# Attention and mixture of experts on one core: w2 loaded in two halves and plain output matmuls, in place of quadrant matmuls

## The chip, the cores and the metric

One core of a Trainium2 chip runs the whole program. The metric is device time in microseconds (us). TensorE (PE; its weight loads are shown as PEld) multiplies matrices into PSUM, VectorE (DVE) and ScalarE (ACT) empty PSUM and do the elementwise work, GpSimd (POOL) issues the loads with its software queue and computes one small power per batch, SyncE (SP) issues the stores.

## What is computed

The input has 8 batches, 8 heads, 576 positions and 64 columns a head. An attention without softmax is normalized and fed to a layer of experts, of which each batch takes exactly one.

```python
kv  = einsum('bhsd,bhse->bhde', k, v)            # 64 x 64 for each head
out = einsum('bhsd,bhde->bhse', q, kv)
x   = out / sqrt(mean(out*out, -1) + 1e-6) * g_norm
x   = heads side by side: (8, 576, 512)
logits = x.mean(1) @ w_gate                      # 8 experts
e      = argmax(logits, 1)                       # one expert for a batch
gate   = softmax(logits)[e]
y      = gate * (relu(x @ w1[e]) @ w2[e])        # w1: 512 x 1024, w2: 1024 x 512
```

With the inputs used here the eight batches choose experts 4, 4, 7, 6, 5, 1, 3, 1. So batches 1 and 7 take weights that are on the chip already.

## The kernel before

All matmuls are in 16-bit floats, cast from 32 bits by the loads. Work is written as steps, and ORDER (L26) lists 367 of them by hand; `emit` (L459) turns each into instructions, and every engine runs its own in that order. A step is named batch, letter, number, and an x for the other of two evacuating engines: 3W1x is step W1 of batch 3. The letters:

- L loads q, k or v of a batch (number 0, 1, 2), 576 KB, on GpSimd's queue (`load_qkv`, L95). Four buffers each.
- T transposes q of a head pair (`s_qt`, L155) into qT; Q (`s_qr`) puts q in another order for that. K makes the 64x64 kv of all heads and casts it into kvb (`s_kv`, L187).
- O computes the attention output of head pairs and squares it on ScalarE; Y copies it from PSUM to the tile o; M takes the mean square with a matmul against constants and ScalarE's reciprocal root; X multiplies everything into xT and sums over positions (`s_x`).
- G0 to G3 do the gate: the logits, the index of the largest (read into a register by GpSimd), the power on GpSimd (L318), the sum and its reciprocal.
- W0 and W1 load w1 and w2 of the expert into one of three slots (`s_w`, L343). From batch 1 on, VectorE first copies the weights from an earlier slot into this one (L354, two halves); from batch 2 on the slot is chosen at run time. The load is then skipped where one of the two batches before had the same expert.
- m0 to m7 are the units of the first layer: 8 matmuls of 288 columns each, and an evacuation with relu to the tile hT (`m_1`, L383). m9 to m16 are halves of the second layer, 4 matmuls of 512 columns, an even number ending a 128-row tile that is scaled and stored (`m_2`, L407, L430). m8 is the last 64 rows, 16 matmuls of 256 columns (L418).
- D is a filler matmul that keeps TensorE's clock up while it would wait (L152). P changes the PSUM pools from the first batch's to the others'.

For batches above 0 O and M treat two head pairs at once (`s_o2`, `s_m2`, `quads`, L215). A pair of heads has a 64x64 kv each, so half of a 128x128 block would be zeros. Here the array is used in four 64x64 quadrants:

```python
for n, rows in ((0, 0), (1, 1), (0, 1), (1, 0)):
    r = slice(64 * rows, 64 * rows + 64)
    for i in range(2):
        e = slice(64 * (rows ^ i), 64 * (rows ^ i) + 64)
        nc.tensor.matmul(outs[n][e, i, 0:HS], lhs(c + n)[r, e],
                         rhs(c + n)[r, i * HS:(i + 1) * HS], start=True, stop=True)
```

The second half of the positions comes out with the two heads swapped, so Y needs three copies (L236 to L238, shown under the helper's line L182), and `s_kv`'s cast (L204) writes each kv twice.

PSUM after batch 0 has two buffers "a" (T, K, O, M, G) and two buffers "m" (the expert layers), two banks each; O and M take both "a" buffers. hT has two buffers. Batch 0 has its own PSUM tags (three "m", two "s") and plain 128x128 matmuls (`s_o`, `s_m`).

Of the kernel before, what the change touches and what calls it, by code (L numbers as in the profile page):

```python
# [24 lines left out]

ORDER = (  # L26
    "0R1x 0R2 0D1 0R0x 0K0 0T0 0T1 0C0 0C1x 0O0 0D1 0D1 0D1 0K1 0K2x 0T3 0C3x 0T2 0O1x "
    "0C2 0K3 0O2 0D1 0M0x 2L0x 0M1x 0M2x 0X0x 0X1x 0O30 0X2 0D1 0D1 2L2x 0M30 0D1 0O31 "
    "0D1 0M31 2L1x 1T0x 0X30x 0X31 1T2 0G1x 0P0 0D1 1T3 1T1 0W0x 1K0 1O0x 3L0 1Y0 0G2x "
    "1Y1x 1M0 2Q0 1X0x 2T0 1O2 1Y3x 1Y2 1X1x 0m0x 2T2x 2T3 3L2 0W1 1M2x 0m4 0G3 1X2x 2K0 "  # L30
    "2T1x 1X3 1G0 0m5 4L0 2O0x 2Y0 0m7 0m3x 1G1 3L1 2Y1x 3Q0 0m2 4L1x 2M0x 4L2 0m1x 3T0x "
    "3T2x 1G2 0m6 2X0x 1W0 2O2 2Y2 1G3 0m13 0m14 1W1x 2Y3x 0m11 3T1x 0m12x 2M2 5L0 1m0 "
    "2X1x 2X2 1m7 2X3x 3K0 3T3x 1m3 2G0 5L1x 1m6 3O0x 3Y0 5L2x 3Y1x 4Q0x 1m2 1m5 4K0 2G1 "
    "1m4 4T0x 2W0 1m1x 3M0 0m8 6L0 4T2x 3X0x 4T3x 0m15 3O2x 3Y2 0m9x 3X1 3Y3x 6L1 0m16x "
    "2G2x 5K0 4T1x 0m10x 6L2x 1m9 2W1x 3M2 2G3 3X2x 1m10x 3X3x 1m8 4O0 4Y1 1m11x 1m12 "
    "4Y0x 2m0x 4M0x 2m3 5Q0x 5T0x 3G0x 2m1 5T1 2m6 5T3x 4X0x 3G1x 2m7 4X1x 1m13x 5T2x 7L0 "
    "1m14x 3W0x 4O2x 4Y2 1m15 4Y3x 1m16x 3G2 6Q0x 2m2 3G3 6K0x 6T0x 3W1x 2m4 2m5 4M2 4X2x "
    "2m11 2m9x 4X3x 6T1x 2m12x 4G0 5O0 5Y0 2m10 5Y1x 2m13 2m14x 4G1 2m15 5M0 4W0x 2m16x "
    "6T2 2m8 5O2 3m0 5Y2 3m1 5X0x 6T3x 3m6 3m7 5Y3 5M2 3m3 3m5 4W1 4G2x 5X1 7L2x 6O0 5X2x "
    "6Y0 3m2x 3m4 6Y1x 5X3 7L1 4m0x 4m1 6M0 7Q0x 4m4x 4G3x 4m5 5G0x 7T0x 4m2 5G1 4m7 6O2x "  # L40
    "3m15x 3m16x 5W0x 3m13 6X0x 6Y2x 3m14 3m11 5W1x 6Y3x 7T2x 3m12 7T3x 6X1 4m3x 6M2 6X2x "
    "5G2x 6X3 6G0x 3m8x 7K0 7T1x 4m6 3m9 3m10 7O0x 7Y0 5G3 4m13x 4m14 4m15 7Y1x 4m16x 6G1 "
    "5m0 5m6 6W0 5m1x 7M0x 4m9 6W1x 6G2x 4m10 5m4x 7O2x 4m8x 7Y2x 5m2x 4m11x 7X0 4m12x "
    "5m7 5m3 7X1x 7Y3 5m5 6m0x 6G3 5m11x 7M2x 7X2x 5m12x 5m9 7X3x 7G0x 5m10 5m15 5m16x "
    "7G1x 6m5 7W0 6m4 5m13x 5m14 7G2x 5m8x 6m6 6m3 7m0 7m6 6m1 7m5 7m7 7m4 7W1 6m2 7m2 "
    "7m3 7G3 6m7 7m1 6m11 6m12x 7m11 7m12 7m15 7m16 7m13 7m14 6m13x 6m14x 7m9 7m10x 6m15 "
    "6m16x 6m9 6m10 6m8 7m8x "
# [4 lines left out]
def kernel(  # L52
# [31 lines left out]
    hp = ctx.enter_context(tc.tile_pool(name="hp", bufs=2))  # L84
# [48 lines left out]
    ones4 = const.tile([P, P], F16)  # L133
    nc.vector.memset(ones4, 1.0 / Dh)
# [20 lines left out]
    def s_qt(b, c, x=False):  # L155
        s = st[b]
        if "qT" not in s:
            s["qT"] = att.tile([P, NP, S], F16, tag="qT", name="qT")
        p32 = psum("s", 2, 1) if first[0] else psum("a")
        pt = p32.bitcast(F16)  # L160
        for j in range(NJ):
            if "qr" in s:
                nc.tensor.transpose(pt[:, 0, j * R:(j + 1) * R], s["qr"][0:R, c, j],  # L163
                                    ident[0:R, 0:R])
                continue
            for i in range(2):
                nc.tensor.transpose(pt[64 * i:64 * i + 64, 0, j * R:(j + 1) * R],
                                    kvq[b][0][0:R, 2 * c + i, j, :], ident[0:R, 0:R])
        s["pt", c] = pt
        if b > 0:  # L170
            s_tc(b, c, x)
# [15 lines left out]
    def s_kv(b, prs):  # L187
        kt, vt = kvq[b][1:3]
        kv = kvb[:, b % 2]
        p32 = psum("s", 2, 1) if first[0] else psum("a")  # L190
        pk = p32[:, 0].rearrange("p (c e) -> p c e", c=NP)
        for c in prs:
            for j in range(NJ):
                for i in range(2):
                    nc.tensor.matmul(pk[64 * i:64 * i + 64, c, 64 * i:64 * i + 64],  # L195
                                     kt[0:R, 2 * c + i, j, :], vt[0:R, 2 * c + i, j, :],
                                     start=(j == 0), stop=(j == NJ - 1))
        cs = slice(prs[0], prs[-1] + 1)
        for i in range(2):
            r = slice(64 * i, 64 * i + 64)  # L200
            if b == 0:
                nc.vector.tensor_copy(kv[r, cs, r], pk[r, cs, r])
            else:
                nc.vector.tensor_copy(  # L204
                    kv[r].rearrange("p c (i e) -> p c i e", i=2),
                    pk[r, :, r].unsqueeze(2).to_broadcast([64, NP, 2, Dh]))
# [5 lines left out]

    def quads(c, outs, lhs, rhs):  # L215
        for n, rows in ((0, 0), (1, 1), (0, 1), (1, 0)):
            r = slice(64 * rows, 64 * rows + 64)
            for i in range(2):
                e = slice(64 * (rows ^ i), 64 * (rows ^ i) + 64)
                nc.tensor.matmul(outs[n][e, i, 0:HS], lhs(c + n)[r, e],  # L220
                                 rhs(c + n)[r, i * HS:(i + 1) * HS], start=True, stop=True)

    def s_o2(b, c):
        s = st[b]
        po = [psum("a") for _ in range(2)]
        quads(c, po, lambda n: kvb[:, b % 2, n, :], lambda n: s["qT"][:, n, :])
        for n in range(2):
            s["sq", c + n] = sm.tile([P, S], F16, tag="sq", name="sq")
            nc.scalar.activation(two(s["sq", c + n]), po[n][:, :, 0:HS], AF.Square)  # L229
            s["po", c + n] = po[n]  # L230

    def s_y(b, c, x):
        s = st[b]
        o = two(sm.tile([P, S], F32, tag="o", name="o"))
        po = s["po", c]
        copy(x, o[:, 0], po[:, 0, 0:HS])  # L236
        copy(x, o[0:64, 1], po[64:128, 1, 0:HS])
        copy(x, o[64:128, 1], po[0:64, 1, 0:HS])  # L238
        s["o", c, None] = o

    def s_m2(b, c):
        s = st[b]
        pm = [psum("a") for _ in range(2)]
        quads(c, pm, lambda n: ones4, lambda n: s["sq", n])
        for n in range(2):
            s["rs", c + n] = sm.tile([P, S], F32, tag="rs", name="rs")
            nc.scalar.activation(two(s["rs", c + n]), pm[n][:, :, 0:HS],  # L247
                                 AF.Abs_reciprocal_sqrt, bias=epsc)

    def s_o(b, c, h=None):  # L250
        s = st[b]
        po = psum("m", 3) if first[0] else psum("a")
        for i in range(2) if h is None else (h,):
            nc.tensor.matmul(po[:, i, 0:HS], kvb[:, b % 2, c, :],
                             s["qT"][:, c, i * HS:(i + 1) * HS], start=True, stop=True)
        po = po[:, :, 0:HS] if h is None else po[:, h:h + 1, 0:HS]
        if not h:
            s["sq", c] = sm.tile([P, S], F16, tag="sq", name="sq")
        nc.scalar.activation(part(s["sq", c], h), po, AF.Square)
        s["o", c, h] = po  # L260

    def s_m(b, c, h=None):
        s = st[b]
        if not h:
            s["rs", c] = sm.tile([P, S], F32, tag="rs", name="rs")
        for hs in ((0,), (1,)) if first[0] and h is None else ((0, 1) if h is None else (h,),):
            pm = psum("s", 2, 1) if first[0] else psum("a")
            for n, i in enumerate(hs):
                nc.tensor.matmul(pm[:, n, 0:HS], ones, s["sq", c][:, i * HS:(i + 1) * HS],  # L269
                                 start=True, stop=True)  # L270
            nc.scalar.activation(two(s["rs", c])[:, hs[0]:hs[-1] + 1], pm[:, 0:len(hs), 0:HS],
                                 AF.Abs_reciprocal_sqrt, bias=epsc)
# [20 lines left out]
    def s_row():  # L293
        s = st[0]
        pg = psum("s", 2, 1)[0:1, 0, 0:E]
# [6 lines left out]
    def s_index(b, pg):  # L302
# [4 lines left out]
        evs.append(nc.gpsimd.value_load(ixs[0:1, b, 0:1], min_val=0, max_val=E - 1))  # L307
# [35 lines left out]
    def s_w(b, i):  # L343
# [3 lines left out]
        if b > 0:  # L347
            if b > 1 and i == 0:
                st[b]["sv"] = nc.vector.value_load(st[b]["src"][0:1, 0:1], min_val=0,
                                                   max_val=NW - 1)  # L350
# [10 lines left out]
        nh = {0: 4, B - 1: 2}.get(b, 1) if i == 0 else 1  # L361
        n = W.shape[3] // nh
        for h in range(nh):
            fs = slice(h * n, (h + 1) * n)
            nc.gpsimd.dma_start(W[:, own, :, fs], (moe_w1, moe_w2)[i][ds(ev, 1), :, fs]  # L365
# [41 lines left out]
    def m_2(b, t, fcs, x=False):  # L407
# [7 lines left out]
        if t == 4:  # L415
# [6 lines left out]
            if last:  # L422
                ot = outp.tile([P, D // 2], F32, tag="ot4", name="ot4")
                scaled(x, ot, po[:, 0, 0:D // 2], b)
                for i in range(2):
                    nc.sync.dma_start(ob[NJ - 1, R - 64:R, i * D // 2:(i + 1) * D // 2],
                                      ot[64 * i:64 * i + 64])
# [31 lines left out]
    def emit(tok):  # L459
# [8 lines left out]
        elif f == "D":  # L468
            warm(psum("s", 2, 1) if first[0] else psum("a"), c)
# [11 lines left out]
        elif f == "C":  # L481
            s_tc(b, c, x)
# [13 lines left out]
        elif f == "Y":  # L496
            s_y(b, c, x)
        elif b > 0 and f in "OM":
            (s_o2 if f == "O" else s_m2)(b, c)
        else:  # L500
            dict(O=s_o, M=s_m, X=s_x)[f](b, c, h)
# [33 lines left out]
```

## Time and profile before

| | us |
|---|---|
| three runs | 209.13, 209.54, 212.11 (median 209.54) |
| the profiled execution | 209.54, its span 207.9 |
| busy in the span: PE, ACT, DVE, POOL | 179.8, 118.6, 118.2, 49.8 |

The span runs from the first instruction to the last; 1.64 us lie around it. A row of a timeline reads: start, duration, engine, line, operation, output<-input, form, count, and in brackets the idle time of the engine before it with what ended it. A row of groups reads: line, engine, operation, names, form, count, busy us, mean ns of one, idle time before them. A row of the chain reads: start, duration, what. PEclk is the clock granted to TensorE, in tenths of full speed or as a share. A busy PE is one with matmuls in flight; since these overlap, the rate is read from a long row of the chain. The DMA queue of the loads moved 26.30 MB, the stores' 10.05 MB with three first loads.

### The profile page before, as it was taken

Reading aid. Unit: us, or ns where it says so; the run is one execution under the profiler, and the core shown is the slowest. Engines: PE = TensorE matmul, PEld = TensorE weight load, DVE = VectorE, ACT = ScalarE, POOL = GpSimd, SP = SyncE. Lnnn points to the kernel's source line nnn. Section 1 sums busy time; section 2 is a strip of 40 time slices with the busy share of each in tenths; the row PEclk is TensorE's granted clock in tenths of the full one; section 3 lists DMA queues with packets and bytes.
Section 4 is the critical chain, followed back from the end, with each engine's and each line's share of the span. In section 5 each row is a group of like instructions: output and inputs, shape, how many; then the busy total and the mean of one; then the engine's idle time right before and its main releaser. Section 6 shows DMA issues by size and latency. Waiting matters only on the chain.

```text
span 207.9 us, 4625 instructions
## 1 busy us (share of the span) xinstructions
PE 179.8 (87%) x1796; PEld 109.9 (53%) x1796; DVE 118.2 (57%) x308; ACT 118.6 (57%) x209; POOL 49.8 (24%) x64
## 2 busy tenths in 40 slices
PE   1678737898999899999898979999949999999990
PEld 0442513576576544667345647474636666874450
DVE  2335456758886778877658785797555367001220
ACT  2437244548878667778676857864624543662120
POOL 7850248002540081024101070140122004000000
PEclk9985855569999999999999999999988999999997
DMA  6999999996999989999999999999999843002554
GB/s 155 195 201 204 203 201 198 204 208 96 165 215 228 181 136 218 252 226 228 230 227 262 231 158 191 186 167 246 252 191 182 177 116 99 20 0 50 146 160 101
DMA packets 37032, 36.94 MB, mean 178 GB/s; under 512 B 2706, under 2 KB 30354, under 8 KB 37010
## 3 DMA queue, kind: packets, MB, share of 16 engines
q0 software_dynamic: 29328, 26.30, 80.6%
q1 hardware_dynamic: 7474, 10.05, 17.0%
q10 hardware_dynamic: 208, 0.29, 0.5%
q8 instruction: 14, 0.23, 0.4%
q14 instruction: 8, 0.07, 0.1%
HBM read 61.88 MB, written 9.44 MB: 343 GB/s over the span
## 4 chain that ended last, share of the span: by engine, by line
PE 47%; DMA 26%; DVE 9%; issue 6%; ACT 6%; POOL 3%; DVEq 0%; POOLq 0%
DMA W<-in_moe_w_dram 23%; PE ps_m L391 18%; PE ps_m L430 16%; DMA vt<-in_v_dram 3%; PE ps_m L418 3%; PE ps_a L220 3%; DVE o L182 3%; PE ps_a L195 2%; PE ps_a L163 2%; DVE W L354 2%; DVE kvb L204 2%; ACT sq L229 1%; ACT rs L247 1%; POOL qt L104 1%; PE ps_s L269 1%
## 5 line engine op out<-in xcount | busy, mean ns | idle before, releaser
L391 PE MATMUL ps_m<-xT,W 128*128 128x288 f16 x512 | 71.6, 294 | 2.1 <-DVE hT L395 1.4
L430 PE MATMUL ps_m<-W,hT 128*128 128x512 f16 x256 | 59.5, 379 | 1.4 <-DMA W<-in_moe_w_dram 0.7
L391 PEld LDWEIGHTS <-W 128*128 128x128 f16 x512 | 49.8, 101 | 19.2 <-issue 4.2
L398 ACT ACTIVATE hT<-ps_m 128x576 f16<-128x576 f32 x51 | 33.1, 650 | 18.3 <-PE ps_m L391 18.1
L430 PEld LDWEIGHTS <-hT 128*128 128x128 f16 x256 | 23.9, 98 | 29.0 <-issue 3.3
L365 POOL DMA_DIRECT2D W<-in_moe_w_dram x20 | 12.5, 626 | 95.3 <-DVE W L354 23.5
L402 ACT ACTIVATE ot<-ps_m,gates 128x512 f32<-128x512 f32 (+1 forms) x22 | 14.3, 649 | 25.0 <-PE ps_m L430 16.4
L404 DVE TENSOR_SCALAR ot<-ps_m,gates 128x512 f32<-128x512 f32 (+1 forms) x18 | 12.4, 688 | 25.8 <-PE ps_m L430 23.5
L354 DVE COPY W<-W 128x2048 f16 (+1 forms) x28 | 19.3, 697 | 12.6 <-DMA W<-in_moe_w_dram 8.4
L182 DVE COPY o<-ps_a 64x288 f32<-64x288 f32 (+1 forms) x42 | 19.1, 455 | 11.3 <-ACT sq L229 10.8
L229 ACT ACTIVATE sq<-ps_a 128x576 f16<-128x576 f32 x28 | 16.6, 649 | 13.8 <-PE ps_a L220 13.8
L247 ACT ACTIVATE rs<-ps_a,epsc 128x576 f32<-128x576 f32 x28 | 19.2, 737 | 9.1 <-PE ps_a L220 9.1
L280 DVE SCALAR_TENSOR_TENSOR xT<-o,gcol,rs 128x576 f16<-128x576 f32 x28 | 22.2, 815 | 3.2 <-ACT rs L247 3.0
L182 ACT COPY o<-ps_a 64x288 f32<-64x288 f32 (+1 forms) x42 | 16.7, 398 | 0.3
L182 ACT COPY qT<-ps_a 128x576 f16<-128x576 f16 x20 | 12.6, 638 | 6.5 <-PE ps_a L163 6.5
L318 POOL TENSOR_TENSOR lg<-base,dl 128x8 f32<-128x8 f32 x8 | 14.1, 1766 | 3.5 <-DVE dl L312 3.3
L395 DVE TENSOR_SCALAR hT<-ps_m 128x576 f16<-128x576 f32 x13 | 9.8, 754 | 6.9 <-PE ps_m L391 6.8
L195 PEld LDWEIGHTS <-kt 96*64 96x64 f16 x384 | 8.7, 125 | 9.4 <-issue 4.6
L163 PE MATMUL ps_a<-ident,qr 96*128 96x96 f16 x144 | 10.9, 218 | 1.8 <-ACT rs L247 1.0
L204 DVE CAST kvb<-ps_a 64x512 f16<-64x512 f32 x14 | 9.6, 687 | 4.3 <-PE ps_a L195 4.2
L163 PEld LDWEIGHTS <-qr 96*128 96x128 f16 x144 | 8.6, 104 | 5.6 <-issue 2.2
L418 PE MATMUL ps_m<-W,hT 128*64 128x256 f16 x128 | 9.2, 293 | 2.7 <-DVE ot L404 2.7
(69 smaller groups left out, 132.0 us busy)
## 6 DMA issues: line engine op xcount, KB each, us to landing
W<-in_moe_w_dram POOLq DMA_DIRECT2D x14, 1024.0 KB, 14.4
out_dram<-ot SPq DMA_DIRECT2D x24, 192.0 KB, 5.3
qt<-in_q_dram POOLq DMA_DIRECT2D x7, 576.0 KB, 13.4
kt<-in_k_dram POOLq DMA_DIRECT2D x7, 576.0 KB, 15.0
vt<-in_v_dram POOLq DMA_DIRECT2D x7, 576.0 KB, 13.4
out_dram<-ot SPq DMA_DIRECT2D x40, 64.0 KB, 5.4
out_dram<-ot SPq DMA_DIRECT2D x16, 128.0 KB, 5.6
W<-in_moe_w_dram POOLq DMA_DIRECT2D x4, 256.0 KB
```

Source lines behind the costliest of these rows:

```text
L163: nc.tensor.transpose(pt[:, 0, j * R:(j + 1) * R], s["qr"][0:R, c, j], ident[0:R, 0:R])
L182: nc.scalar.copy(out, in_) if x else nc.vector.tensor_copy(out, in_)
L229: nc.scalar.activation(two(s["sq", c + n]), po[n][:, :, 0:HS], AF.Square)
L247: nc.scalar.activation(two(s["rs", c + n]), pm[n][:, :, 0:HS], AF.Abs_reciprocal_sqrt, bias=epsc)
L280: nc.vector.scalar_tensor_tensor(out=part(s["xT"][:, c, :], h), in0=s["o", c, h], scalar=gcol, in1=part(s["rs", c], h), op0=ALU.mult, op1= ...
L318: nc.gpsimd.tensor_tensor(lg, base, st[b]["dl"], ALU.pow)
L354: nc.vector.tensor_copy(W[:, own, h * n:(h + 1) * n], W[:, ds(sv, 1), h * n:(h + 1) * n].rearrange("p o c f -> p (o c) f"))
L391: nc.tensor.matmul(ph[:, i, 0:HS], w1[:, c, fb * P:(fb + 1) * P], s["xT"][:, c, i * HS:(i + 1) * HS], start=(c == 0), stop=(c == 3))
L398: nc.scalar.activation(two(s["hT"][:, fb, :]), ph[:, :, 0:HS], AF.Relu)
L402: nc.scalar.activation(out, in_, AF.Copy, scale=gates[:, b:b + 1])
L418: nc.tensor.matmul(po[64 * i:64 * i + 64, 0, 0:D // 2], s["hT"][:, fc, 4 * P:S], w2[:, fc, i * D // 2:(i + 1) * D // 2], start=(fc == 0), ...
L430: nc.tensor.matmul(po[:, 0, :], s["hT"][:, fc, t * P:(t + 1) * P], w2[:, fc, :], start=(fc == 0), stop=(fc == 7))
```

## The change

The two kernels differ in more than the loading of w2: each has its own variant and its own ORDER.

- w2 is loaded in two transfers, each half of the 1024 rows (`i == 1` in `s_w`); w1 is loaded as before.
- `quads`, `s_o2`, `s_m2`, `s_y` and the constants ones4 are gone. O and M take one head pair for all batches, with two 128x128 matmuls of 288 columns on a kv block that has zeros outside its two 64x64 parts. Above batch 0, O copies its output in one 128x576 copy from PSUM to o. The cast of kv writes each head once.
- ORDER has 374 steps, with 17 fillers instead of 10, and other positions. Second-layer units of one batch are all ahead of the first-layer units of the next; before, those of batches 6 and 7 were mixed.
- hT has one buffer.
- Batch 0's PSUM tags are "t" and "kv" (a bank each), "m" (two of two banks) and "p" (one of two banks); M of a half pair uses the bank of "t" or "kv". C always copies on VectorE.
- The two register loads leave out the check of bounds at run time.
- The last piece of the last batch is stored by the queues of SP and ACT, one each.

```diff
-    hp = ctx.enter_context(tc.tile_pool(name="hp", bufs=2))
+    hp = ctx.enter_context(tc.tile_pool(name="hp", bufs=1))
...
-        for i in range(2):
-            r = slice(64 * i, 64 * i + 64)
-            if b == 0:
-                nc.vector.tensor_copy(kv[r, cs, r], pk[r, cs, r])
-            else:
-                nc.vector.tensor_copy(
-                    kv[r].rearrange("p c (i e) -> p c i e", i=2),
-                    pk[r, :, r].unsqueeze(2).to_broadcast([64, NP, 2, Dh]))
+        nc.vector.tensor_copy(kv[0:64, cs, 0:64], pk[0:64, cs, 0:64])
+        nc.vector.tensor_copy(kv[64:128, cs, 64:128], pk[64:128, cs, 64:128])
...
+    def s_o(b, c, h=None, x=False):
+        s = st[b]
+        po = (psum("p", 1) if h == 1 else psum("m")) if first[0] else psum("a")
         for i in range(2) if h is None else (h,):
             nc.tensor.matmul(po[:, i, 0:HS], kvb[:, b % 2, c, :],
                              s["qT"][:, c, i * HS:(i + 1) * HS], start=True, stop=True)
...
         nc.scalar.activation(part(s["sq", c], h), po, AF.Square)
+        if b > 0:
+            o = two(sm.tile([P, S], F32, tag="o", name="o"))
+            copy(x, o, po)
+            po = o
         s["o", c, h] = po
...
+        pm = (psum("p", 1) if h is None else psum("tkv"[h:2 * h + 1], 1, 1)) if first[0] \
+            else psum("a")
+        for i in range(2) if h is None else (h,):
+            nc.tensor.matmul(pm[:, i if h is None else 0, 0:HS], ones,
+                             s["sq", c][:, i * HS:(i + 1) * HS], start=True, stop=True)
...
-        evs.append(nc.gpsimd.value_load(ixs[0:1, b, 0:1], min_val=0, max_val=E - 1))
+        evs.append(nc.values_load(
+            ixs[0:1, b, 0:1], engines=(mybir.EngineType.Pool,), min_val=0, max_val=E - 1,
+            skip_runtime_bounds_check_because="it is the index of the largest of E values"))
...
-        nh = {0: 4, B - 1: 2}.get(b, 1) if i == 0 else 1
+        if i == 1:
+            for h in range(2):
+                cs = slice(4 * h, 4 * h + 4)
+                nc.gpsimd.dma_start(W[:, own, cs], moe_w2[ds(ev, 1), h * F // 2:(h + 1) * F // 2]
+                                    .rearrange("o (c p) d -> p (o c) d", p=P), cond=cond)
+            return
+        nh = {0: 4, B - 1: 2}.get(b, 1)
...
-                    nc.sync.dma_start(ob[NJ - 1, R - 64:R, i * D // 2:(i + 1) * D // 2],
-                                      ot[64 * i:64 * i + 64])
+                    eng = nc.scalar if i and b == B - 1 else nc.sync
+                    eng.dma_start(ob[NJ - 1, R - 64:R, i * D // 2:(i + 1) * D // 2],
+                                  ot[64 * i:64 * i + 64])
```

The new ORDER around the steps that the prediction speaks of (the end of batch 0's attention, and where batches 3 to 6 take their weights):

```
0W0x 2L1x 0P0x 0D1 1T1 1T2 1T3 0D1 0D1 0D1 0D1 0D1 0W1 0D1 2Q0x 0D1 0G2x 1K0 2T0x 1O0 1O2
1M0 0G3 0m0 2T2 1O1 0m3x 3L0x 3L1 1M1 1X0x 1O3 0m4 0m5 1X1 1M2 1M3x 0m1 1X2 0m7 ...
...
6L1x 2m5 5T0 4M3 3W0x 2m1 2m2 3G2x 4X1x
...
5O0x 2m9x 6L2x 3W1 2m10x 2m15x 2m16x 5O1 4G0 5T2x 6Q0 5M0x 2m11x 2m12x 4G1 3m0 6T0x 7L0x
3m5 6T1x 4W0 3m7x 3m6 5X0x 6T2x
...
4W1x 5X3x 3m12 6O0 5G0x
...
6O2 4m4 5W0x 6X0x 4m3 6O3 5G3 5W1x 4m6 6M2x 4m9x
...
6G1x 5m0 5m4x 6W0 6G2x 5m7
...
5m12x 6W1 5m15x 7M2x 5m16x 7M1 5m8
```

## The prediction

> **What bounds the kernel now.** I read the busy slices first, then windows of the span, then the timeline where a window falls short, then the chain and the groups.
>
> ```profile
> PE   1678737898999899999898979999949999999990
> ...
> PEclk9985855569999999999999999999988999999997
> DMA  6999999996999989999999999999999843002554
> ```
>
> TensorE is the bound, except for its first fifth, where it runs at half clock, and for a notch in slice 30. The DMA engines are full until slice 31: loads are nearly as scarce as matmuls. The same by stage (after the stretch: busy PE, PEld, DVE, ACT, POOL, then granted clock, DMA share, GB/s):
>
> ```profile
> 24.72:45.20 20.48, 15.39 (x177) 9.57 (x177) 11.67 (x29) 9.21 (x17) 7.93 (x9) 0.50 1.34 202
> ...
> 151.00:158.00 7.00, 4.26 (x37) 2.94 (x35) 2.71 (x4) 2.32 (x5) 2.56 (x2) 0.76 1.06 206
> 158.00:203.20 45.20, 45.11 (x318) 27.85 (x315) 15.10 (x36) 18.72 (x31) 2.10 (x4) 1.00 0.45 101
> ```
>
> From 158 us on TensorE works through a backlog without a gap (45.11 of 45.20), so whatever lets it reach that point earlier shortens the time one for one. What is lost lies in the half-clock stretch before 45.2 and in the notch. The notch in the timeline:
>
> ```profile
> 151.73 0.44 PE L220 MATMUL ps_a<-qT,kvb 64*64 64x288 f16 x8
> ...
> 152.77 1.42 DVE L354 COPY W<-W 128x2048 f16 x2 [3.21 <-DMA W<-in_moe_w_dram]
> 154.10 0.75 DVE L404 TENSOR_SCALAR ot<-ps_m,gates 128x512 f32<-128x512 f32 x1
> 154.90 1.92 PE L418 MATMUL ps_m<-W,hT 128*64 128x256 f16 x16 [2.74 <-DVE ot L404]
> ```
>
> Step 6W1 copies w2 from a slot chosen at run time, so it waits for 5W1's load. VectorE runs in order: behind the copy stand the evacuation of an output tile and that of a hidden tile, so TensorE's two "m" buffers stay full and it waits 2.97 us from one matmul's end to the next start. The clock then falls to half for one window of 3.4 us (0.76 over the 7 us): another 1.7 us. That load took this long, and the backlog runs at these rates:
>
> ```profile
> 135.90 16.84 DMA W<-in_moe_w_dram
> ...
> 174.54 12.85 PE ps_m L391 x104
> 187.39 13.81 PE ps_m L430 x64
> ```
>
> So one 288-column matmul at full clock is 12.85/104 = 123.6 ns and a 512-column one 215.8 ns. (The 294 and 379 ns of the groups are latencies of overlapped matmuls.)
>
> **The change part by part.**
>
> *Quadrants removed.* What does a quadrant group cost TensorE's stream?
>
> ```profile
> 116.38 2.13 PE L391 MATMUL ps_m<-xT,W 128*128 128x288 f16 x16
> ...
> 118.44 0.44 PE L220 MATMUL ps_a<-qT,kvb 64*64 64x288 f16 x8
> ...
> 118.82 2.13 PE L391 MATMUL ps_m<-xT,W 128*128 128x288 f16 x16
> ```
>
> From start to start of the plain groups 2.44 us pass; 16 x 123.6 = 1.98 are theirs, so eight quadrant matmuls cost 0.46 us, most of it entering and leaving the mode. The plain form is four 128x288 matmuls, 0.49 us. Over 28 groups (7 batches x 2 pairs x output and mean square) removal costs 28 x 0.03 = **+0.8 us**. Bounds: 0 (the same) and 28 x (0.49 - 0.37) = 3.4, if only the 0.37 us between 118.44 and 118.82 counted; I take 0.8, since the start-to-start row holds all of it.
>
> The Trainium skill, page "TensorEngine Tiling (Array Packing)", sections Tiling Modes and Theoretical Speedup, speaks against this part: four independent 64x64 tiles, up to 2x per small dimension. By it, as an estimate, a group would take a quarter of eight plain matmuls, 0.25 us, and removing 28 would cost 6.8 us instead of 0.8; its own remark that a change of mode drains the array is what the row shows.
>
> *Evacuation.* Three copies a head pair become one:
>
> ```profile
> L182 DVE COPY o<-ps_a 64x288 f32<-64x288 f32 (+1 forms) x42 | 19.1, 455 | 11.3 <-ACT sq L229 10.8
> ...
> L182 ACT COPY o<-ps_a 64x288 f32<-64x288 f32 (+1 forms) x42 | 16.7, 398 | 0.3
> ...
> L395 DVE TENSOR_SCALAR hT<-ps_m 128x576 f16<-128x576 f32 x13 | 9.8, 754 | 6.9 <-PE ps_m L391 6.8
> ...
> L204 DVE CAST kvb<-ps_a 64x512 f16<-64x512 f32 x14 | 9.6, 687 | 4.3 <-PE ps_a L195 4.2
> ```
>
> The copies take 19.1 + 16.7 = 35.8 us. The nearest rows for one 128x576 copy are L395 (0.75) and ScalarE's L398 (0.65): 20 x 0.75 + 8 x 0.65 = 20.2 instead of 35.8 us. The kv casts halve in width: from 0.22 us for 64 columns (L202) and 0.69 for 512, 256 cost 0.42, so 5.9 instead of 9.6 us. This is off the critical path (both engines are 57% busy); its worth is in PSUM. A pair held both "a" buffers for squares and copies (1.19 + 1.22 us to the end); one head pair holds one for 0.65 + 0.75. Stalls over 0.2 us for such reasons (48, 51, 57, 72, 85 us and others) sum to about 5 us after 45 us; I take **-0.5**, because the single steps also come more often. Bounds: -3 and +14 (see the third rival).
>
> *New order, middle.* I sum matmul durations between a load's step and the first step that needs it, before and after, in us of matmul work. Where the profile waits: 5W1 to copy 6W1, 16.2 becomes 21.8; 3W0 to copy 4W0, 14.2 becomes 15.7; 3W1 to 4W1, 19.1 becomes 21.2; 4W0 to its first use, 11.9 becomes 17.1. Shorter: 5W0 to first use 14.5 to 12.4; 4W1 to copy 5W1 14.0 to 13.2; 3W0 to first use 16.7 to 13.0. A load lands 8.5 (least) to 16.8 us after issue; 1 MB alone takes 5.2 us at the 202 GB/s above. What stands ahead in the new queue is one q, k or v load (576 KB, 2.9 us) or none, so I expect 8.5 to 10.5 us, 2.5 to 4 us of slack at the shortest. Then the notch (2.97 + 1.7) goes, and with it the waits at 99.06 us (0.97, w2 landing) and at 120.67 us (1.54: VectorE behind copy 4W1). That is 7.2; I keep 1.2 for new small waits: **-6.0**. Bounds: -7.2 and -1.3 (a notch of 4.7 comes back). If the cover is gone, the price is that notch.
>
> *w2 in halves.* GpSimd issues eight more loads, 0.77 to 0.9 us each for the six batches that load, 0.04 for the two whose expert is already there: 5 us on an engine 24% busy, whose next work is qkv loads and the power L318. Units on the first half can start 2.6 us sooner; nobody waits there in the sum. **0**; bounds -1 and +1. On GpSimd's queue 0W0 now stands ahead of 2L1 and 0W1 ahead of batch 3's loads: w2 of batch 0 lands some 5 us sooner, k of batch 2 some 5 us later, at about 37 us, where 2K0 comes after 45. SP's queue keeps its order of outputs.
>
> The Trainium skill, page "DMA: Bandwidth & Descriptors", section Anatomy of one DMA, speaks against it: about 2.0 us fixed per transfer. By it, as an estimate, six more transfers would add 12 us to the queue. Here queued loads run at 195 to 206 GB/s in every slice from 5 to 45 us whatever their size (144 to 1024 KB), so no fixed part shows.
>
> *Front and warm-up.* The first batch has other PSUM tags and squares sooner: step by step (last v at 13.85 us, q of batch 1 at about 17, two half-pairs in separate banks) I reach the index 0.4 us earlier, and the loads without bounds checks save 0.2 us each. Seven more filler matmuls, six of them ahead of 1K0, push 1K0 from 24.7 to about 28 us at 0.45 us each. But from 1K0 to the first expert unit 0m0 it took 10.4 us (24.66 to 35.10); with single steps it is K 1.5, casts 0.85, output 0.5, square 0.65, copy 0.75, mean 0.5: 5 us. So 0m0 starts at 33 instead of 35.1, the next unit at 36 instead of 39.8, and TensorE is dense from there, so the clock may rise one or two windows before 45.2. **-2.0**; bounds +3.1 (seven fillers, nothing regained) and -5 (clock up at 38.4).
>
> *Smaller.* hT has one buffer, so the first evacuation of batch b+1 waits for the last second-layer matmul of b; it stands behind that in TensorE's order anyway: 0, else one evacuation, 0.75 us a batch. The bounds checks leave VectorE (0.2 us x 6): 0. The last output piece goes on ACT's queue beside SP's: four SP issues take 2.39 us at the end, one is saved: **-0.6**.
>
> Sum on the profiled execution: 207.9 + 0.8 - 0.5 - 6.0 + 0 - 2.0 - 0.6 = 199.6 us of span. It lasted 209.54, which is the median too; with the 1.64 around the span the forecast is **201.2 us**.
>
> **The rivals.**
>
> 1. *A load is late elsewhere.* 3W0 or 5W0 misses its unit, or 5W1's copy blocks VectorE. For: DMA is at 9 tenths, slack 2.5 to 4 us. Against: less stands ahead of each than before. One notch: 201.2 + 4.7 = 205.9.
> 2. *Quadrants were worth their face value* (0.25 instead of 0.46): 201.2 + 28 x 0.21 = 207.1. Against: the start-to-start row. Or the front gives 3.1 up instead of gaining 2.0: 206.3.
> 3. *Slower: single steps starve on PSUM.* 56 output and mean steps take one of two "a" buffers each; an output step holds it 1.4 us. Where less matmul work than this lies before the next but one, TensorE stalls some 0.5 us. With 28 stalls: 201.2 + 14 = 215. It decides from 25 stalls (12.5 us). Against: the new order puts a unit of 0.99 us between most; I find some ten too short.
> 4. *The clock rises at 38.4 us and nothing new waits*: 201.2 - 3 - 1.2 = 197.
> 5. *The change does nothing*: no; every gain here is from waits of the old order, but if they all return, 209.
>
> **How the numbers follow.** Forecast 0.46 (own range 198.5 to 204.5), rival 1 0.20, rival 2 with the front 0.12, rival 3 0.12, rival 4 0.10; rival 5 lies within 1 and 2. About 2%, 4.2 us, is what a measurement of this kernel can tell from no change, so faster means under 205.3: forecast, rival 4 and a fifth of rival 1, 0.60. Slower means over 213.7: rival 3, 0.12. The rest, 0.28, is the same. The range reaches from 197 over rivals 1 and 2 to 208.5, leaving out rival 3 and a little at both ends.
>
> **What would show it.** No DVE wait for a W load beyond 1 us and no notch in PE after 100 us; granted clock up before 45.2 us; 28 fewer mode changes at equal TensorE pace; o copies near 20 us in all. I am wrong if half clock lasts beyond 50 us, if PE waits for W, or if it waits for "a" buffers in more than ten places.

## The result, and the profile after

| | median us | runs | ratio to the kernel before |
|---|---|---|---|
| before | 209.33 | 4, 207.31 to 212.11 | 1 |
| after | 196.0 | 4, 194.46 to 198.61 | 0.937 [0.925, 0.949] |
| after, on another chip | 196.69 | 6, 193.38 to 197.36 | 0.940 [0.931, 0.949] |

The kernel became 6.3% faster. The direction was forecast, but the time lies 1 us below the range's low end and 5 us below the forecast. Ratios here leave out the executions that took over 1.5% longer than the fastest of the same kernel (the profiled one of after and four of the six on the other chip among them), while medians hold all. The profiled execution of after is the longest of its four (198.61 us, span 197.0) and has the lowest mean clock of them, 0.954 against 0.982 to 1.0: TensorE's clock was half from 21.97 to 39.03 us in it, and its front is read with that in mind.

The busy slices of the profile after, then the windows that were read before (stretch: busy PE, PEld, DVE, ACT, POOL, then granted clock, DMA share, GB/s):

```profile
PE   0277799799899999999989999999999999999991
...
PEclk9999755599999999999999999999999999999999
DMA  6999999999999999999999999999999899063035
```

```profile
24.72:45.20 20.48, 18.66 (x170) 12.23 (x171) 10.82 (x26) 8.07 (x13) 9.32 (x11) 0.65 1.27 190
...
98.00:122.00 24.00, 23.42 (x237) 15.82 (x235) 16.44 (x42) 14.94 (x25) 8.76 (x9) 1.00 1.20 226
...
151.00:158.00 7.00, 7.00 (x51) 3.94 (x49) 3.52 (x7) 4.87 (x8) 1.53 (x2) 1.00 0.92 167
```

The notch is gone: in 151 to 158 us TensorE is busy for 7.00 us instead of 4.26, at full clock. The same stretch of the middle in the kernel before shows that more than the notch went: from 98 to 122 us TensorE was busy for 21.23 us, now for 23.42.

```profile
98.00:122.00 24.00, 21.23 (x188) 12.23 (x186) 16.48 (x41) 17.44 (x31) 4.43 (x5) 1.00 1.14 228
```

All waits of TensorE between 45 us and the end of after that are put down to data or buffers (what waits, for what, us in total, times, longest):

```profile
PE ps_a L224 <- DVE o L179: 0.9, 2, 0.5
PE ps_m L358 <- DMA W<-in_moe_w_dram: 0.8, 1, 0.8
PE ps_a L207 <- DVE o L179: 0.5, 1, 0.5
```

Before, the longest of these waits, and that of VectorE's copies of weights, were:

```profile
PE ps_m L418 <- DVE ot L404: 2.7, 1, 2.7
PE ps_m L391 <- DVE hT L395: 1.4, 1, 1.4
PE ps_m L430 <- DMA W<-in_moe_w_dram: 0.7, 1, 0.7
PE ps_a L195 <- issue: 0.7, 2, 0.4
PE ps_a L220 <- DVE qT L182: 0.6, 1, 0.6
```

```profile
DVE W L354 <- DMA W<-in_moe_w_dram: 8.4, 4, 3.2
```

After, one weight load is still late, by 0.8 us, and three waits of about half a microsecond are for the copy of the output out of PSUM. VectorE's copies of weights, which waited 8.4 us for landings before, start without such a wait now; one in the timeline:

```profile
116.87 1.42 DVE L315 COPY W<-W 128x2048 f16 x2
```

To see where the time came from I counted the matmul work done by fixed moments: matmuls started by then, times the full-clock prices of the prediction (all work: 160.6 us before, 161.4 with plain matmuls). One profiled execution each; the kernels of the experiments are there for later. The prices are not exact: the last kernel does 106.1 us of work in the 105.8 between 45.2 and 151 us.

| us of work done by | 45.2 us | 98 us | 151 us | TensorE's end | span |
|---|---|---|---|---|---|
| before | 13.9 | 63.4 | 112.9 | 203.1 | 207.9 |
| after | 15.4 | 68.0 | 119.9 | 193.0 | 197.0 |
| before, plain matmuls and one copy | 17.4 | 66.3 | 116.0 | 196.7 | 201.5 |
| the same with three copies | 16.2 | 65.0 | 114.7 | 198.2 | 203.0 |
| before, plain, no weight copies | 19.3 | 70.0 | 120.9 | 191.7 | 196.7 |
| after, without seven fillers | 19.5 | 72.0 | 125.6 | 187.3 | 191.3 |

Between 45.2 and 151 us, 105.8 us of time, before does 99.0 us of work and after 104.5. So the old middle was 7 us short of what TensorE can do, and the new one 1.3 us.

The first column depends on the execution too. The profiled one of before has a mean clock of 0.921, while the runs of before beside the experiments have medians near 0.95, so part of its late start may be its own. Two more profiled executions speak for the new order: the changed kernel's second (196.61 us, on the other chip) and that with w2 in one transfer (195.29 us, below) are ahead of before by about 4.6 and 5.3 us of work at 45.2 us, and do about 4.7 and 5.7 us more than it between 45.2 and 151.

The other count is of what TensorE loses after 45 us: the stalls over 0.2 us, each the time from one matmul's start to the next less its full-clock price. A stall is put to late weights where TensorE waits for a load, or for VectorE while that works without a pause behind a copy that waited for one.

| us of stalls after 45 us | late weights | others |
|---|---|---|
| before | 6.3 | 5.1 |
| after | 1.1 | 2.1 |
| after, on another chip | 2.2 | 2.1 |
| before, plain matmuls and one copy | 6.2 | 2.1 |
| the same with three copies | 3.0 | 4.0 |

Before lost another 1.7 us to the half clock behind its notch.

### The profile page after: what moved, and what is told of

It is laid out like the page before. It is cut to its first block, busy times and chain, and to the rows that moved or that the text cites. A ratio compares the mean times of both kernels' runs of the same rounds, so it can differ in the third digit from the quotient of the medians.

```text
span 197.0 us, 4393 instructions
## 1 busy us (share of the span) xinstructions
PE 176.1 (89%) x1691; PEld 115.9 (59%) x1691; DVE 111.4 (57%) x289; ACT 106.6 (54%) x168; POOL 54.3 (28%) x72
## 4 chain that ended last, share of the span: by engine, by line
PE 74%; DMA 13%; DVE 4%; ACT 4%; issue 2%; POOL 0%; DVEq 0%; POOLq 0%; ACTq 0%
PE ps_m L358 30%; PE ps_m L398 24%; DMA W<-in_moe_w_dram 5%; DMA qt<-in_q_dram 4%; DMA kt<-in_k_dram 4%; PE ps_a L224 3%; PE ps_a L207 3%; PE ps_a L160 3%; ACT sq L212 3%; PE ps_a L192 3%; DVE o L179 3%; PE ps_m L385 2%; PE ps_a L149 2%; PE ps_kv L149 1%; DVE W L315 1%
## 5 line engine op out<-in xcount | busy, mean ns | idle before, releaser
L358 PE MATMUL ps_m<-xT,W 128*128 128x288 f16 x512 | 69.3, 289 | 0.8 <-DMA W<-in_moe_w_dram 0.8
L369 ACT ACTIVATE ot<-ps_m,gates 128x512 f32<-128x512 f32 (+1 forms) x26 | 17.0, 655 | 18.1 <-PE ps_m L398 11.7
L228 ACT ACTIVATE rs<-ps_a,epsc 128x576 f32<-128x576 f32 x28 | 20.5, 740 | 7.5 <-PE ps_a L224 7.5
L179 DVE COPY o<-ps_a 128x576 f32<-128x576 f32 x20 | 15.0, 756 | 14.6 <-ACT sq L212 14.3
L315 DVE COPY W<-W 128x2048 f16 (+1 forms) x28 | 19.3, 695 | 1.4 <-DVE src L296 0.5
L371 DVE TENSOR_SCALAR ot<-ps_m,gates 128x512 f32<-128x512 f32 (+1 forms) x14 | 9.4, 673 | 18.4 <-PE ps_m L398 16.6
L325 POOL DMA_DIRECT2D W<-in_moe_w_dram x16 | 9.2, 577 | 36.0 <-PE ps_m L398 16.6
L332 POOL DMA_DIRECT2D W<-in_moe_w_dram x12 | 7.0, 588 | 38.8 <-PE ps_m L358 14.7
L179 ACT COPY qT<-ps_a 128x576 f16<-128x576 f16 x15 | 9.5, 636 | 14.2 <-PE ps_a L160 14.2
L224 PE MATMUL ps_a<-sq,ones 128*128 128x288 f16 x56 | 11.3, 291 | 2.0 <-DVE o L179 1.9
L207 PE MATMUL ps_a<-qT,kvb 128*128 128x288 f16 x56 | 11.9, 302 | 1.1 <-DVE o L179 0.7
L224 PEld LDWEIGHTS <-ones 128*128 128x128 f16 x64 | 6.1, 100 | 8.0 <-issue 3.2
```

The source lines that it names most:

```text
L179: nc.scalar.copy(out, in_) if x else nc.vector.tensor_copy(out, in_)
L207: nc.tensor.matmul(po[:, i, 0:HS], kvb[:, b % 2, c, :], s["qT"][:, c, i * HS:(i + 1) * HS], start=True, stop=True)
L224: nc.tensor.matmul(pm[:, i if h is None else 0, 0:HS], ones, s["sq", c][:, i * HS:(i + 1) * HS], start=True, stop=True)
L228: nc.scalar.activation(part(s["rs", c], h), pm[:, 0:2 if h is None else 1, 0:HS], AF.Abs_reciprocal_sqrt, bias=epsc)
L315: nc.vector.tensor_copy(W[:, own, h * n:(h + 1) * n], W[:, ds(sv, 1), h * n:(h + 1) * n].rearrange("p o c f -> p (o c) f"))
L358: nc.tensor.matmul(ph[:, i, 0:HS], w1[:, c, fb * P:(fb + 1) * P], s["xT"][:, c, i * HS:(i + 1) * HS], start=(c == 0), stop=(c == 3))
```

## The experiments

The theories were these. *Late loads*: the time came from the new order, in which copies and matmuls no longer wait for weights; copies on VectorE spread the wait to others. *Form*: it came from the plain matmuls with a lighter evacuation, whatever the order. *Clock*: it came from TensorE's clock rising sooner, through fillers or a denser front. And the part that the change is named after, w2 in halves, might be worth something by itself. Ratios are to the kernel before on the same chip.

**The named part: w2 in one transfer again** (after, edited).

```diff
-            for h in range(2):
-                cs = slice(4 * h, 4 * h + 4)
+            for h in range(1):
+                cs = slice(0, 8)
```

> The changed kernel with w2 of each batch in one transfer, as before. The forecast gave the halves nothing: 196.0 within 1 us. Rival: units on the first half start 2.6 us sooner and the copies behind half a load wait less, so one transfer costs 2 to 4 us: 198 to 200. Other rival, a fixed 2 us per transfer: 12 us less queue time, a gain of 1 us or more where TensorE waits for a load at 142 us.

Measured: 196.8 us (194.37 to 198.42), against 196.0 (194.46 to 198.61) and 196.69 (193.38 to 197.36) for the changed kernel itself. Loading w2 in two halves makes no difference that these runs can tell.

**Old order without the copies of weights on VectorE** (before, edited; it leaves out the copies of batches 2 to 6, whose result the inputs used here never need, since these batches all load).

```diff
-            for h in range(2):
+            for h in range(2 if b in (1, B - 1) else 0):
```

> The kernel before without VectorE's copies of weights for batches 2 to 6 (ten pairs of copies of 0.70 us less, 14 us of VectorE work; with these inputs none of those batches repeats an expert, so the copies carry nothing that is used). Theory A, late loads hold VectorE: the waits of the copies for landing loads at 98, 107, 116 and 149.5 us (8.4 us in sum) no longer stand ahead of evacuations; the notch at 152 us with its half clock goes. 209.3 - 6 to -8 = about 202. Theory B, the middle was gained by lighter evacuation (one copy of 128x576 instead of three, one PSUM buffer held instead of two): only VectorE's relief shows, 209.3 - 2 = 207.

Measured: 204.03 us, 0.980 [0.970, 0.990]: some 4 us faster, less than the 6 to 8 of the late loads and more than the 2 of the form. The notch is gone (first fence), but with no copy to wait, TensorE itself now waits for the same kind of load (second fence, the timeline):

```profile
151.00:158.00 7.00, 7.00 (x61) 4.97 (x58) 3.81 (x9) 4.88 (x10) 0.00 (x0) 1.00 1.13 206
```

```profile
121.01 2.13 PE L391 MATMUL ps_m<-xT,W 128*128 128x288 f16 x16 [1.81 <-DMA W<-in_moe_w_dram]
```

So the copies made the late loads dearer, but the loads are late without them too.

**New order without these copies** (after, the same edit; it leaves out the same).

> The changed kernel without the copies of batches 2 to 6 (with these inputs they carry nothing that is used). Theory A: its profile shows one wait on a weight load in the middle (0.99 us at 142 us, TensorE itself, not behind VectorE), so nothing is left to gain: within 1 us of 196.0. Theory B says the same within 2 us. If it gains over 3 us, copies still cost in the new order and A is wrong about where they stopped costing.

Measured: 195.4 us, 0.942 [0.933, 0.950]. No gain that can be told: no copy waits for a load in the new order.

**Old order with plain matmuls and one copy** (before, edited: in `s_o2` and `s_m2`, and the kv cast and `s_y`).

```diff
-        quads(c, po, lambda n: kvb[:, b % 2, n, :], lambda n: s["qT"][:, n, :])
+        for n in range(2):
+            for i in range(2):
+                nc.tensor.matmul(po[n][:, i, 0:HS], kvb[:, b % 2, c + n, :],
+                                 s["qT"][:, c + n, i * HS:(i + 1) * HS], start=True, stop=True)
...
-        copy(x, o[:, 0], po[:, 0, 0:HS])
-        copy(x, o[0:64, 1], po[64:128, 1, 0:HS])
-        copy(x, o[64:128, 1], po[0:64, 1, 0:HS])
+        copy(x, o, po[:, :, 0:HS])
```

> The kernel before with its own order and its pairs, but with plain 128x128 matmuls for output and mean square, one 128x576 copy for three, and kv cast once. TensorE pays 28 x 0.03 = 0.8 us. Theory A: the late loads stay, so the time does too: 209.3 +0.8 -0.5 to -2, some 208.5. Theory B: the gain of the middle comes along: 209.3 - 3 or more, 206 or less. Rival (quadrants at face value, 0.25 us a group): 209.3 + 6, 215.

Measured: 202.67 us, 0.971 [0.962, 0.979], about 6 us faster with the old order. By the table of work (one execution each), 3.5 us of it are gained by 45.2 us; the clock rises for good at 38.47 us instead of 45.2. The middle gains nothing (98.6 us of work in it, 99.0 before), since the notch now falls into it, and the rest comes after 151 us. By the stalls, those for late weights stay (6.2 us) and the others fall from 5.1 to 2.1. The loads are as late as ever, with new places to wait at:

```profile
PE ps_m L429 <- DMA W<-in_moe_w_dram: 2.2, 1, 2.2
PE ps_m L390 <- DVE xT L279: 1.9, 1, 1.9
PE ps_m L417 <- DVE ot L403: 1.6, 1, 1.6
```

The second and third stand behind a waiting weight copy on VectorE. The third is the notch itself, now before 151 us, shorter and without a fall of the clock:

```profile
147.73 1.42 DVE L353 COPY W<-W 128x2048 f16 x2 [2.35 <-DMA W<-in_moe_w_dram]
149.07 0.74 DVE L403 TENSOR_SCALAR ot<-ps_m,gates 128x512 f32<-128x512 f32 x1
...
149.86 1.06 PE L417 MATMUL ps_m<-W,hT 128*64 128x256 f16 x16 [1.59 <-DVE ot L403]
```

**The same, but with three copies a head pair** (`copy(x, o[:, 0], ...)` and two copies of 64 rows, from the rows where the plain form has them). This parts the evacuation from the matmuls.

> The old order with plain matmuls and kv cast once, but still three copies from PSUM for each head pair. It splits the 5.6 us that the plain form gave. If the three copies and the buffers they hold were the cause (theory B): back to about 207. If leaving the quadrant mode or the halved casts were: it stays near 203. By the steps of the prediction, the first stretch needs 0.5 to 0.65 us less for each pair's copies, twice on the way to 0m0: I expect 204.5.

Measured: 204.11 us, 0.988 [0.981, 0.996]. So both parts of the form gain: the one copy in place of three, and the plain matmuls with the narrower cast of kv, which the two kernels share. How much is whose is not settled: the ratios put the copies at 1.7% of 2.9% (the two intervals do not meet, but come from two chips), the medians at 1.4 us (204.11 less 202.67) and the profiled spans at 1.5, of which the table of work shows 1.2 by 45.2 us. In the stalls of the two profiled executions, three copies lose 4.0 us outside the late weights, one copy 2.1.

**Each quadrant group twice** (before, edited; it repeats work and changes no value). This prices the quadrant mode.

```diff
-        for n, rows in ((0, 0), (1, 1), (0, 1), (1, 0)):
+        for n, rows in 2 * ((0, 0), (1, 1), (0, 1), (1, 0)):
```

> The kernel before with each group of eight quadrant matmuls issued twice in a row (sixteen, the same result): it prices the quadrant matmuls apart from entering and leaving the mode. If the prediction's reading holds (most of the 0.46 us is the change of mode), eight more inside the mode cost eight steps of the 157 ns seen for seven steps plus the second wave, 0.24 us: 28 x 0.24 = 7 at most, less where TensorE waits: 209 + 4 to 7. Rival, 0.46 us is the price of the matmuls themselves: 28 x 0.46 = 13, 221.

Measured: 207.95 us, 1.008 [1.004, 1.012]. In the timeline a group now has 16 matmuls:

```profile
116.41 2.13 PE L391 MATMUL ps_m<-xT,W 128*128 128x288 f16 x16
118.48 0.68 PE L220 MATMUL ps_a<-qT,kvb 64*64 64x288 f16 x16
119.09 2.13 PE L391 MATMUL ps_m<-xT,W 128*128 128x288 f16 x16
```

2.68 us pass from plain group to plain group; less 16 x 123.6 ns that is 0.70 us (0.71 over all groups), where eight matmuls took 0.46. Eight quadrant matmuls by themselves are 0.245 us, and going into the mode and out of it 0.22 us. The surprise is the total: 28 x 0.245 = 6.9 us of added TensorE work cost 0.8%, 1.7 us (at most 2.5 by the interval; 1.0 by the medians, 207.95 against 206.94). The work filled time in which TensorE had been waiting: between 45.20 and 151 us it was busy for 103.28 us instead of 100.02, and its stalls after 45 us sum to 4.5 us instead of the 11.4 before. Nor does a better clock show that could have paid for it: over the executions that the ratio is taken from, the mean clock has a median of 0.946, and 0.949 in the kernel before on the same chip. The weight copies on VectorE, which now come later, waited only 4.4 us instead of 8.4, and the notch did not come:

```profile
DVE W L354 <- DMA W<-in_moe_w_dram: 4.4, 4, 1.4
```

A kernel that TensorE alone bounds in its middle could not do that.

**Both: old order, plain form, no weight copies.**

> The old order with plain matmuls and light evacuation, and without the weight copies of batches 2 to 6 (which carry nothing that is used with these inputs). Alone the two edits gave 5.6 and 4.2 us. If one acts in the first 45 us and in keeping the clock up, the other on late loads behind VectorE, they add up but for the 1.7 us of half clock that both remove: 208.2 - 8 = 200. What then is left to the new kernel (196) is the order of the middle, the fillers and the end: some 4 us. Rival, both remove the same waits: 202.

Measured: 199.31 us, 0.967 [0.959, 0.974]. The two gains, 2.0% and 2.9%, should give 4.9% if they were independent; it is 3.3% (the interval of the form alone, 0.962 to 0.979, holds it). So in part they remove the same waits.

**Plain old order with half of each load of weights of batches 2 to 6** (it leaves out the second half of w1 and of w2, so these units compute with old weights; the number of matmuls is the same). This asks directly what late loads cost, those of q, k and v behind them included.

```diff
+            if 1 < b < B - 1:
+                fs = slice(0, n // 2)
```

> The old order with plain matmuls and light evacuation (0.971 of before), and only half of each weight load of batches 2 to 6 (the other half is left out, so what is multiplied there is old data): 5 MB, some 26 us of the load queue less. Theory A, what this order still loses after 45 us is late loads (waits on a weight load of 2.4 us at 94, 2.1 at 116 and 1.8 at 148 us in its profile): 202.7 - 5 to -6, 0.945 of before. Rival, the order of the attention steps against the expert units: it stays at 0.965 to 0.971.

Measured: 197.17 us, 0.953 [0.947, 0.959], 1.8% below the plain old order with whole loads. The middle does 104.6 us of work, as the changed kernel's does. No wait of TensorE for weights is left:

```profile
PE ps_a L195 <- DMA vt<-in_v_dram: 0.6, 1, 0.6
```

**The changed kernel with the same halves left out.**

> The changed kernel with the same halves of weight loads left out. Theory A: its order has loads early enough, only waits of up to 1 us are left: 196.0 - 0 to -1. Rival, loads bound the new order as well, only less: 3 us or more.

Measured: 194.73 us, 0.935 [0.926, 0.945], against 0.937 and 0.940 for the whole loads. In the new order the loads cost no time that can be told: 1 us at most by the ratios, though intervals of 1% either way could hide 2.

**Fewer fillers** (after, without seven of the eight between 0P0 and 1K0), **the same again, and no fillers at all** (all 17 left out, which stand ahead of 1K0; they compute nothing that is used).

```diff
-    "0X30 0D1 0D1 0X31x 0G1x 0W0x 2L1x 0P0x 0D1 1T1 1T2 1T3 0D1 0D1 0D1 0D1 0D1 0W1 0D1 "
-    "2Q0x 0D1 0G2x 1K0 2T0x 1O0 1O2 1M0 0G3 0m0 2T2 1O1 0m3x 3L0x 3L1 1M1 1X0x 1O3 0m4 "
+    "0X30 0D1 0D1 0X31x 0G1x 0W0x 2L1x 0P0x 0D1 1T1 1T2 1T3 0W1 "
+    "2Q0x 0G2x 1K0 2T0x 1O0 1O2 1M0 0G3 0m0 2T2 1O1 0m3x 3L0x 3L1 1M1 1X0x 1O3 0m4 "
```

> The changed kernel without seven of its eight filler matmuls between the first batch's attention and 1K0. Theory C, fillers hold the clock: TensorE falls to half clock from about 22 to 42 us in every run, 2 to 5 us slower than 196.0. Rival, the fillers only push 1K0 back (it comes at 31.0 us in the profile, 27.8 where the clock was up): without them 1K0 comes 2 to 3 us sooner and the time falls by 1 to 3 us.

> The changed kernel without seven fillers ahead of 1K0, once more: if they only push 1K0 back, 1 us under the changed kernel on the same chip; if they hold the clock, 1 us or more above it.

> The changed kernel without any of its 17 filler matmuls. Without seven of them it took 195.0, no slower. Theory C, fillers hold the clock up: half clock from the start to about 40 us, 198 to 200. Rival, the chain of batch 0 and 1 bounds the first 35 us and TensorE's clock matters little there: 194 to 196.

Measured: 194.96 us, 0.947 [0.938, 0.955]; again 195.44 us, 0.942 [0.936, 0.948]; without any 194.87 us, 0.944 [0.936, 0.952]. The changed kernel, run again on the chip of the second of these:

> The changed kernel itself, beside the next one on one chip: 0.94 of before, 195 to 196.

Measured: 196.69 us, 0.940 [0.931, 0.949]. Fillers neither bring the gain nor cost any of it that can be told. Whether a denser front brings some of it through an earlier clock was not tried by itself.

**The smaller parts undone** (after, with the bounds checks back, two hT buffers, and the last piece stored by SP alone).

> The changed kernel with its small parts undone: run-time bounds checks back, hT with two buffers, the last piece stored by SP alone. The forecast gave the store 0.6 us and the others nothing: 196.0 + 0.6, at most +1.5 if the checks (0.2 us each, twice a batch, behind them the weight copies) lie on a path.

Measured: 196.89 us, 0.947 [0.938, 0.957]. These parts are worth 0.7% to 1.0% by the ratios, and as the interval holds the changed kernel's ratio, this is not settled.

**Some of these parts on the old order** (plain, no weight copies, with loads of registers unchecked and the last piece on two queues).

> The old order with plain matmuls, without the weight copies of batches 2 to 6, and with the new kernel's small parts (unchecked register loads, last piece stored by two queues). Without the small parts it took 0.967 of before. If the small parts are worth what undoing them in the new kernel cost (1 us at most): 0.962 to 0.965. Then 4 us up to the new kernel belong to the order alone. If they carry more of the rest: 0.955 or less.

Measured: 198.64 us, 0.959 [0.953, 0.966], where 0.967 [0.959, 0.974] was without them. The intervals overlap: under 1%, not settled.

No version was clearly faster than the changed kernel.

## Why the prediction was wrong in size

The step that failed is the worth of the lighter evacuation. The sum has it at -0.5 us, as off the critical path; the stalls that it stands for fell by 3.0 us, and together with the plain matmuls it gave about 6 us in the old order, where the sum has +0.8 - 0.5. The other miss is the front, whose size changes from one execution to the next.

*The bound (failed in part).* "TensorE is the bound, except for its first fifth" and the notch held from 158 us on, where the backlog is. From 45 to 151 us it held only in the main. TensorE was busy there in nine slices of ten, but 3.3 us went to late weights and 5.1 to other stalls. Doubling the quadrant groups showed that 6.9 us more work cost 1.7 us, and halving the loads of the plain old order gave 1.8%.

*Quadrants removed, +0.8 (right).* The mode's price is 0.46 us a group as read, of which 0.22 is entering and leaving: about half, and not "most of it". The plain form is 0.49:

```profile
43.01 0.49 PE ps_a L224 x4
```

The Trainium skill, page "TensorEngine Tiling (Array Packing)", section Key Properties, says that a change of tiling mode drains TensorE, without a price; the doubled groups give it here, 0.22 us. Without that, the eight quadrant matmuls (0.245 us) would have been twice as fast as the plain four.

*Evacuation, -0.5 (the step that failed).* The copies fell from 35.8 us to 20.1, where 20.2 was worked out:

```profile
L179 DVE COPY o<-ps_a 128x576 f32<-128x576 f32 x20 | 15.0, 756 | 14.6 <-ACT sq L212 14.3
```

```profile
L179 ACT COPY o<-ps_a 128x576 f32<-128x576 f32 x8 | 5.1, 635 | 0.0
```

What they are worth was mis-sized. The prediction found about 5 us of TensorE's stalls after 45 us that go back to buffers of PSUM and took 0.5 of them. By the count of stalls outside late weights, they were 5.1 us and are 2.1 after, in both profiled executions, so the term measures -3.0 us, its own bound. It is the form that does it: in one profiled execution each, the old order with plain matmuls has 4.0 with three copies and 2.1 with one. Plain matmuls and light evacuation, +0.8 - 0.5 = +0.3 in the sum, gave 2.9%, about 6 us, by themselves in the old order, of which one copy for three is between 1.4 us and over half. What goes beyond the stalls I had called "off the critical path". By the table of work (one execution each) it was on the path in two more places: in the chain of batch 1's attention, which decides when the dense stretch begins, and around the notch, where VectorE's queue is what TensorE waits for. The prediction had both places, but as gains of the order.

*New order, middle, -6.0 (right in size).* The waits that it names, 7.2 us with the half clock, are gone. Kept back for new ones was 1.2 us; one late load, at 143.14 us, cost 1.1 in the first profiled execution of after, and two cost 2.2 in the second. One wait more went than listed, 0.82 us from 110.2 us on, behind the copy of weights before it:

```profile
109.22 1.42 DVE L354 COPY W<-W 128x2048 f16 x2 [1.94 <-DMA W<-in_moe_w_dram]
...
111.06 0.43 PE L220 MATMUL ps_a<-qT,kvb 64*64 64x288 f16 x6 [0.56 <-DVE qT L182]
```

Middle and evacuation together: from 45.2 us to TensorE's end after is ahead by 9.4 us by the work done, where -6.0 - 0.5 was forecast (by the stalls, 7.2 + 0.8 - 1.1 + 3.0 = 9.9). How this divides into order and form is read from the kinds of stall and not proven, since halving the loads, leaving out the copies and the plain form remove in part the same waits. By the runs, form alone gives 2.9%, and order with batch 0's PSUM tags and the smaller parts another 3% (0.971 to 0.937 and 0.940).

In these two profiles the loads themselves do not come sooner: the last weights land at 167.95 us before and at 168.55 after (164.96 in the second execution of after, whose front is ahead too). That the new order has other matmuls ready meanwhile is how I read it.

*w2 in halves, 0 (right).* No difference could be measured, and nothing like the 12 us that the prediction set against it.

*Front and warm-up, -2.0 (right in its chain, wrong in its clock).* From 1K0 to 0m0 5.07 us pass, 5 were worked out (10.4 before). All seven added fillers stand ahead of 1K0, not six. 1K0 came at 31.0 us and not at 28, so 0m0 started at 36.0, later than before, and still TensorE was 1.5 us ahead by 45.2 us. But that is the execution in which the clock was half until 39.03. In the second one of the changed kernel it was full from 29.3 us, and TensorE was some 4.6 us ahead. In the profiled executions of six edited kernels of the new order 17.5 to 20.2 us of work were done by 45.2 us instead of 13.9: nearer the bound of -5 than the -2.0 taken, though measured from an execution of before whose clock was low. The profiled execution of after (198.61) is 2.6 us under the forecast, and the median another 2.6 under that; that this second part is the clock's is argued from these figures, not shown.

*Smaller, -0.6 (right).* From the end of TensorE to the end of the span 4.76 us became 4.0, with the last pieces on two queues:

```profile
193.01 0.47 ACT L369 ACTIVATE ot<-ps_m,gates 128x256 f32<-128x256 f32 x1 [0.26 <-PE ps_m L385]
193.51 0.56 ACTq L394 DMA_DIRECT2D out_dram<-ot  x1
193.66 0.47 SPq L394 DMA_DIRECT2D out_dram<-ot  x1
```

In sum, for the profiled execution: +0.8 for the matmuls, -1.5 front, -9.4 from there to TensorE's end, -0.75 at the end, -10.9 in all (207.9 to 197.0), where -8.3 was forecast.

*The rivals and the range.* Rival 4, an earlier clock and no new waits at 197 us, is nearest to what happened, at a chance of 0.10. Rivals 1 to 3 did not come: one load is late by 0.8 us, no quadrant was worth its face value, and three waits for "a" buffers, not 28, are left. The low end, 197.0, was rival 4 itself, as if nothing could go better than the named waits; but the bounds of the terms reached lower (-3 for the evacuation, -5 for the front, -7.2 for the middle), and the range should have taken them in.

## What to carry to other kernels

A TensorE that is busy in nine tenths of the slices may still lose time to loads and buffers: look at whether work added to it costs its full price, before pricing what is removed from it. An in-order engine that runs a copy with a run-time source is a place where a late load turns into stalls of everything queued behind, so an evacuation in that queue is on the path however idle the engine is on average. Parts that remove the same wait do not add up: price them together, and let the range's good end reach to the sum of the good bounds.

## What was not expected of the hardware

- Work added to TensorE cost a quarter of its price: 6.9 us more for 1.7. In the profiled execution of it the clock rose for good at 38.99 us instead of 45.2, and the fall at the notch did not come, but over all executions the mean clock is that of the kernel before (medians 0.946 and 0.949), so the clock is not what paid, as far as such means can tell. When it falls after a stall, as in the notch before, it is back after 3.41 us. The Trainium skill, page "TensorE: Matmul & The Clock Gate", section "Part 1: The HAM clock gate (the "warmup" mystery)", gives a free-running window of about 3.4 us; the length of the fall in the notch agrees.
- The mean granted clock of an execution can read too high. The changed kernel without fillers shows 0.997, but its timeline has eight matmuls of 288 columns in 2.12 us at 32.6 us, and sixteen in the same time at 37.3, so the clock was half in the first stretch:

```profile
32.58 2.12 PE L358 MATMUL ps_m<-xT,W 128*128 128x288 f16 x8
...
37.34 2.12 PE L358 MATMUL ps_m<-xT,W 128*128 128x288 f16 x16
```

- Fillers meant to keep the clock up in the first 30 us are worth nothing that can be told: without them the whole is as fast (194.87 against 196.0 and 196.69 us). Nor did they hold it: with all 17 the clock was half from 21.97 to 39.03 us in one execution, and without any it was half in the first stretch and full from 35.33. Why, was not tried further.
